# Attention through agents and a cosine layer, one core: first output products of a chunk one step later; in the last batch, half a step's copy behind the next cosine, linear products and the transposition's copy apart

## The chip, the cores and the metric

One of the cores of a Trainium2 chip runs the whole program. It has TensorE (PE, matrix products, written to PSUM), VectorE (DVE), ScalarE (ACT), GpSimd (POOL) and a queue that starts transfers (SP); each works through its own instructions in order and waits on semaphores for the others. GpSimd has no operand in PSUM anywhere in this kernel. The metric is the device time in microseconds (us) of one execution. Before the change it was 1162.13 us, the median of three runs (1161.17 to 1162.33).

## The reference

```python
scale = 1 / sqrt(128)                                   # B = 4 batches, N = 12480 tokens, C = 128
a2k   = softmax(scale * agents @ k.T)                   # 49 agents to all tokens
q2a   = softmax(scale * q @ agents.T)                   # every token to 49 agents
x     = (q2a @ (a2k @ v)).reshape(49920, 128)
h     = x @ w_in                                        # 128 -> 2048
out   = (h * cos(h)) @ w_out                            # 2048 -> 128
```

## The kernel before, in words

The 49920 tokens are 52 groups of 960 (`GRP`), 13 to a batch (`NG`), each of two chunks of 480 tokens (`CH`). For a chunk the 2048 inner columns are taken in 8 pieces of 256 (`NP` = 8), so there are 832 steps (`NSTEP`), 208 to a batch (`PER`). This text writes i = 0 to 7 for a step's place in its chunk and o for its place in its batch. What bounds the time is the loop over these steps (line 1165).

A step n does this. TensorE makes h for 256 columns, two products `ph<-pT,a` of 480 columns (line 1175; `a` already holds w_in multiplied by the agents' values, `pT` the tokens' softmax weights, transposed). ScalarE writes the cosine of it to `c` (line 1178). VectorE makes r = (c - 1) * h (line 1197), one instruction of 960 elements in each partition. Four steps later (`LAG` = 4) TensorE multiplies r by w_out, two products `po<-r,w` (line 1217), which add up over the chunk's 8 steps. Because r lacks h itself, the chunk's last step also adds two linear products `po<-pT,b` (lines 1213 and 1214). Then ScalarE copies the sum out, `osb<-po` (line 1226). So in the steps of the next chunk ScalarE's order is: cosine of i=3, the copy `osb<-po`, cosine of i=4.

Buffers: `ph` has three (line 618), so the h of a step may be made when the r of three steps before is done. `c` has three (`CB`), so a cosine waits until the readers of the cosine three steps before are done. `r` has six. `po` has one (line 624): the first product of a chunk waits until `osb<-po` of the chunk before has read it.

Beside this loop runs other work, which a planner puts into steps (`plan`, lines 1137 to 1153): scores of the next batch, values, projections, and in every step at most one such job on TensorE; the single buffer `one` takes their results. For each group `query_turned` (line 769) transposes the softmax weights: four products `one<-ident,p`, a copy `p<-one` on ScalarE (line 774), then on GpSimd two pairs `pT<-p` (a cast) and `pT<-p,pT` (a subtraction) for the two chunks.

In batches 0 to 2 these jobs fill TensorE and VectorE. The last batch has fewer of them. There, 23 steps (`asides`, line 1155; i = 0 of the batch's chunks, except near its two softmax bursts at o = 8 and o = 96) split their r: VectorE makes the first half (line 1190), ScalarE copies the second half of h out of PSUM to `raw` (line 1189), and GpSimd makes the second half of r from it in two instructions, a product and a subtraction (lines 1191 and 1192).

The order on each engine is the order of the code (`ordered`).

Of the kernel before, what the change touches and what calls it, by code (L numbers as in the profile page):

```python
# [9 lines left out]
F32 = mybir.dt.float32  # L10
F32R = mybir.dt.float32r
I32 = mybir.dt.int32
U32 = mybir.dt.uint32
AF = mybir.ActivationFunctionType
ALU = mybir.AluOpType
# [3 lines left out]
P = 128  # L19
# [3 lines left out]
CH = TT * HT  # L23
# [19 lines left out]
NV = 5  # L43
WL = 19
TL = 12
SH = 1
AD = 2
KB = 24
# [70 lines left out]
X1 = 208  # L119
XB = 1  # L120
XC = 3
XO = 1
N0 = 2
N1 = 4
N2 = 2
# [19 lines left out]
def agent_attention_cos_ffn(ctx, tc, qT, kT, v, agT, w_in, w_out, outT):  # L145
    nc = tc.nc
    NB, _, N = qT.shape
# [6 lines left out]
    NF = DFF // P  # L154
    NP = NF // 2
    NG = N // GRP
# [6 lines left out]
    looping = [False]  # L163
    wide_at = set()
    ordered = [False]
    step = [0]
    STEP = NCH * NP
    PER = NG * STEP
# [19 lines left out]
    pe, dve, act, pool = (Ordered(x) for x in (nc.tensor, nc.vector, nc.scalar, nc.gpsimd))  # L188
# [14 lines left out]
    w1 = const.tile([P, NF, P], F32R, name="w1")  # L203
# [412 lines left out]
    with ExitStack() as pools:  # L616
        sb = pools.enter_context(tc.tile_pool(name="sb", bufs=2))
# [3 lines left out]
        def small():  # L621
            return ps_1.tile([P, 512], F32, name="one")
# [11 lines left out]
        b1 = [sb.tile([KR, P], F32R, name=f"b1{i}", bufs=1) for i in range(2)]  # L634
        b2 = [sb.tile([KR, P], F32R, name=f"b2{i}", bufs=1) for i in range(2)]

        pTs = [sb.tile([KR, NCH, CH], F32R, name=f"pT_{i}", bufs=1) for i in range(3)]
# [19 lines left out]
        NSTEP = NB * PER  # L657
# [111 lines left out]
        def query_turned(n, lone=0):  # L769
            pt = small()  # L770
            for t in range(HT):
                pe.transpose(pt[:KR, t * TT:(t + 1) * TT], p_in[n % 2][:, t, :KR], ident[:TT, :TT])
            p = sb.tile([KR, CH], F32, name="p")
            act.copy(p, pt[:KR, :CH])
            pT = pTs[n % 3]
            for c, (own, other) in enumerate((half_rows, half_rows[::-1])):
                if lone:
                    act.copy(pT[own, c], p[own])
                else:
                    pool.tensor_copy(pT[own, c], p[own])  # L780
                (dve if lone else pool).tensor_sub(pT[other, c], p[own], pT[own, c].bitcast(F32))
# [223 lines left out]
        plan, post = Plan(), Plan()  # L1005
# [3 lines left out]
        def job(n, *parts, by=10 ** 6):  # L1009

            queue.append((n, len(queue), by, parts))
# [58 lines left out]
        for n in range(1, NQ):  # L1070
            plan(max(1, n * STEP - WL), query_weights, n)
            job(max(2, n * STEP - TL), (query_turned, n), by=n * STEP - TL + 6)

# [6 lines left out]
        early = [pieces[2 * b + 2] for b in range(NB)]  # L1080
# [3 lines left out]
        for b in range(NB):  # L1084
            o = b * PER
            go, stop = o + (T1 if b < NB - 1 else T3), o + PER + T2
# [28 lines left out]
            for g in range(NG):  # L1115
                plan(k1 + 16 + SH * g, nxt.shift, g, 1, pool)
            burst(go, early[b], late[b][:N1], nxt)
# [9 lines left out]
            i = (b + 1) % 2  # L1127
# [11 lines left out]
        while queue or begun:  # L1139
# [4 lines left out]
            x = min(ready, key=lambda x: (x[2], x[1]))  # L1144
            if x is not begun:
                queue.remove(x)
            n, i, by, parts = x
# [7 lines left out]
        def asides(n):  # L1155

            b, o = n // PER, n % PER
            if n < XA or n > NSTEP - 6 or any(x in shut for x in range(n - XB, n + XC)):
                return False
            if b == NB - 1:  # L1160
                return n % XL in XK and not T3 <= o < T3 + XZ
            return X0 <= o < X1 and n % XL in XP

        rs = {}
        for n in range(NSTEP + LAG):
            pinned[0] = n < NP
            looping[0] = True
            step[0] = n
            if n < NSTEP:
                q, c, i = n // STEP, n // NP % NCH, n % NP  # L1170
                ai = a[q // NG % 2]
                ph = ps_h.tile([P, 2, 512], F32, name="ph")
                for j in range(2):
                    f = slice((2 * i + j) * P, (2 * i + j + 1) * P)
                    pe.matmul(ph[:, j, :CH], ai[:, f], pTs[q % 3][:, c], start=True, stop=True)
                h = ph[:, :, :CH]
                cos = sb.tile([P, 2, CH], F32, name="c", bufs=CB)
                act.activation(cos, h, AF.Sin, bias=HALF_PI, scale=1.0)
                aside = asides(n)
                if aside and XO == 0:  # L1180
                    hs = sb.tile([P, 512, 2], U32, name="raw", bufs=2).rearrange("p x t -> p (x t)").bitcast(F32)[:, :2 * CH].rearrange("p (j x) -> p j x", j=2)
                    act.copy(hs[:, 0], h[:, 1])
            plan.run(n)
            if n < NSTEP:
                r = rs[n] = sb.tile([P, 2, CH], F32R, name="r", bufs=RB)
                if aside:
                    if XO:
                        hs = sb.tile([P, 512, 2], U32, name="raw", bufs=2).rearrange("p x t -> p (x t)").bitcast(F32)[:, :2 * CH].rearrange("p (j x) -> p j x", j=2)
                        act.copy(hs[:, 0], h[:, 1])
                    dve.scalar_tensor_tensor(r[:, 0], cos[:, 0], 1.0, h[:, 0], op0=ALU.subtract, op1=ALU.mult)  # L1190
                    pool.tensor_mul(hs[:, 1], cos[:, 1], hs[:, 0])
                    pool.tensor_sub(r[:, 1], hs[:, 1], hs[:, 0])
                elif TS and n == NSTEP - 1:
                    for j in range(2):
                        dve.scalar_tensor_tensor(r[:, j], cos[:, j], 1.0, h[:, j], op0=ALU.subtract, op1=ALU.mult)
                else:
                    dve.scalar_tensor_tensor(r, cos, 1.0, h, op0=ALU.subtract, op1=ALU.mult)
            while tails:
                f, args = tails.pop(0)
                f(*args)  # L1200
            post.run(n)
            m = n - LAG
            if m < 0:
                continue
            q, c, i = m // STEP, m // NP % NCH, m % NP
            if i == 0:
                if c == 0:
                    osb = sb.tile([P, GRP], F32, name="osb", bufs=2)
                po = ps_o.tile([P, 512], F32, name="po")[:, :CH]
            r = rs.pop(m)  # L1210
            if i == NP - 1:
                k = q // NG % 2
                pe.matmul(po, b1[k], pTs[q % 3][:, c], start=False, stop=False)
                pe.matmul(po, b2[k], pTs[q % 3][:, c], start=False, stop=False)
            for j in range(2):
                f = 2 * i + j
                pe.matmul(po, w1[:, f, :], r[:, j, :], start=(f == 0), stop=(f == NF - 1))
            if i == NP - 1:
                at = q * GRP
                if TS and m == NSTEP - 1:  # L1220
                    for on, copy, x in ((nc.sync, act.copy, 0), (nc.scalar, dve.tensor_copy, CH // 2)):
                        part = slice(c * CH + x, c * CH + x + CH // 2)
                        copy(osb[:, part], po[:, x:x + CH // 2])
                        on.dma_start(outT[:, at + part.start:at + part.stop], osb[:, part])
                    continue
                act.copy(osb[:, c * CH:(c + 1) * CH], po)
                if q == NQ - 1:
                    nc.sync.dma_start(outT[:, at + c * CH:at + (c + 1) * CH], osb[:, c * CH:(c + 1) * CH])
                elif c == NCH - 1:
                    nc.sync.dma_start(outT[:, at:at + GRP], osb)  # L1230
# [5 lines left out]
        pt = small()  # L1236
# [10 lines left out]
    with tc.If(far):  # L1247
        with ExitStack() as pools:
            sb = pools.enter_context(tc.tile_pool(name="gsb", bufs=2))
# [8 lines left out]
            p = sb.tile([TT, HT, 2 * HI], F32, name="p", bufs=1)  # L1258
# [64 lines left out]
            for b in range(NB):  # L1323
# [13 lines left out]
                for c in range(DFF // 512):  # L1337
# [5 lines left out]
                                                   op0=ALU.mult, op1=ALU.subtract)  # L1343
# [36 lines left out]
```

## Time and profile before

| what | us |
|---|---|
| median of the runs | 1162.13 |
| the profiled execution | 1160.97 |
| span in its trace | 1159.2 |
| TensorE busy | 1118.7 |
| VectorE busy | 1064.4 |
| ScalarE busy | 977.2 |
| GpSimd busy | 564.2 |

The span runs from the first instruction of the trace to the last; what lies around it is 1.8 us. A busy time counts an instruction from start to end, and two that overlap in an engine's pipeline are counted once. The granted clock of TensorE was 0.998 over the span.

### The profile page before, as it was taken

To read this page: it belongs to the slowest core of one execution; us is meant where nothing else is said; L and a number is where in the kernel's file an instruction comes from. 1 tells how busy PE (TensorE), PEld (TensorE's weight loads), DVE (VectorE), ACT (ScalarE), POOL (GpSimd) and SP (SyncE) were. 2 spreads that over 40 slices of the span, in tenths; PEclk is the share of its full clock that TensorE was granted. 3 is DMA by queue.
4 is the path that set the end of the run, shared out by engine and by line. 5 is a ranking of instruction groups with operands and counts; after the bars stand their busy time and mean duration, and the time that the engine had idled before them with its cause. 6 is when DMAs were issued, how large, how long until landed. Compare 5 with 4: busy or idle time off the path is not lost.

```text
span 1159.2 us, 17231 instructions
## 1 busy us (share of the span) xinstructions
PE 1118.7 (97%) x6075; PEld 924.1 (80%) x6075; DVE 1064.4 (92%) x1201; ACT 977.2 (84%) x1268; POOL 564.2 (49%) x726
## 2 busy tenths in 40 slices
PE   9989999999999999999999999999999999999996
PEld 8869888878887888877887888887888777767774
DVE  5888989999998999989999999998999899999996
ACT  3568877889889888898888887888988999999996
POOL 2013313678964122559893331366896455535551
PEclk9999999999999999999999999999999999999999
DMA  8734342143332232233331332224331100000001
GB/s 331 308 141 136 104 130 92 57 148 101 99 106 68 85 103 86 86 104 106 107 108 53 110 96 86 86 68 139 108 107 52 35 18 35 34 18 35 18 35 38
DMA packets 31631, 109.44 MB, mean 94 GB/s; under 512 B 3504, under 2 KB 4016, under 8 KB 31536
## 3 DMA queue, kind: packets, MB, share of 16 engines
q1 hardware_dynamic: 31392, 108.13, 28.7%
q8 instruction: 50, 0.82, 0.3%
q14 instruction: 45, 0.37, 0.1%
q10 hardware_dynamic: 144, 0.12, 0.0%
HBM read 82.68 MB, written 25.56 MB: 93 GB/s over the span
## 4 chain that ended last, share of the span: by engine, by line
PE 62%; DVE 21%; ACT 11%; issue 4%; POOL 1%; DMA 0%; ACTq 0%; DVEq 0%
PE ph L182 27%; PE po L182 23%; DVE r L182 15%; PE one L182 12%; ACT c L182 6%; DVE rz L182 2%; ACT osb L182 2%; DVE e L182 1%; DVE mx L182 1%; ACT p L182 1%; DVE sums L182 1%; ACT s L182 1%; ACT e L182 1%; ACT L182 1%; DVE s L182 1%
## 5 line engine op out<-in xcount | busy, mean ns | idle before, releaser
L182 DVE SCALAR_TENSOR_TENSOR r<-c,ph 128x960 fp32r<-128x960 f32 (+1 forms) x833 | 907.4, 1132 | 49.1 <-ACT c L182 41.8
L182 ACT ACTIVATE c<-ph 128x960 f32<-128x960 f32 x832 | 783.5, 977 | 132.8 <-PE ph L182 122.5
L182 PE MATMUL ph<-pT,a 113*128 113x480 f32 x1664 | 517.1, 392 | 16.3 <-DVE r L182 12.6
L182 PE MATMUL po<-r,w 128*128 128x480 f32 x1664 | 523.8, 396 | 5.6 <-ACT osb L182 5.3
L182 PEld LDWEIGHTS ph<-pT,a 113*128 113x128 f32 x1664 | 296.7, 189 | 123.0 <-DVE r L182 60.9
L182 PEld LDWEIGHTS po<-r,w 128*128 128x128 f32 x1664 | 291.8, 189 | 52.7 <-ACT osb L182 14.8
L182 POOL CAST pT<-p 49x480 fp32r<-49x480 f32 x102 | 59.2, 580 | 282.6 <-ACT p L182 279.8
L182 PEld LDWEIGHTS one<-ag,xt 128*120 128x120 f32 x1088 | 134.7, 184 | 11.3 <-DVE sums L182 1.5
L182 PE MATMUL one<-ag,xt 128*120 128x98 f32 x1088 | 134.2, 265 | 0.7 <-DVE b L182 0.4
L182 POOL TENSOR_TENSOR pT<-p,pT 49x480 fp32r<-49x480 f32 x102 | 124.1, 1217 | 8.2
L182 POOL TENSOR_TENSOR vh<-vt,vh 120x512 fp32r<-120x512 f32 x78 | 93.3, 1196 | 30.6 <-ACT vh L182 30.6
L182 POOL TENSOR_TENSOR p<-e,rz 120x392 f32<-120x392 f32 x51 | 43.5, 853 | 48.1 <-DVE rz L182 47.0
L182 PE MATMUL po<-pT,b 113*128 113x480 f32 x208 | 62.4, 381 | 0.0
L182 POOL TENSOR_TENSOR raw<-c,raw 128x480 f32<-128x480 f32 x23 | 28.3, 1229 | 70.0 <-ACT raw L182 69.9
L182 ACT COPY osb<-po 128x480 f32<-128x480 f32 x104 | 58.1, 559 | 2.2 <-PE po L182 2.2
L182 PEld LDWEIGHTS ph<-ag,xt 128*120 128x120 f32 x480 | 53.1, 188 | 7.5 <-DVE r L182 4.4
L182 PE MATMUL ph<-ag,xt 128*120 128x98 f32 x480 | 55.4, 272 | 3.1 <-DVE r L182 2.0
L182 POOL TENSOR_TENSOR e<-e,mx 120x392 f32<-120x392 f32 x26 | 21.9, 843 | 71.0 <-DVE mx L182 71.0
L182 PEld LDWEIGHTS one<-vh,eh 120*113 120x113 f32 x312 | 45.9, 177 | 8.2 <-POOL vh L182 2.5
L182 PE MATMUL one<-vh,eh 120*113 120x258 f32 x312 | 50.7, 284 | 1.4 <-DVE e L182 0.9
L182 POOL TENSOR_TENSOR eh<-s,eh 120x196 fp32r<-120x196 f32 x78 | 47.6, 610 | 6.3
L182 PEld LDWEIGHTS po<-pT,b 113*128 113x128 f32 x208 | 38.8, 188 | 6.0
(137 smaller groups left out, 725.4 us busy)
## 6 DMA issues: line engine op xcount, KB each, us to landing
xt<-qT SPq DMA_DIRECT2D x52, 480.0 KB, 3.5
outT<-osb SPq DMA_DIRECT2D x51, 480.0 KB, 2.8
xt<-kT SPq DMA_DIRECT2D x46, 480.0 KB, 3.7
vt<-v SPq DMA_DIRECT2D x43, 512.0 KB, 3.7
c<-kT SPq DMA_DIRECT2D x6, 480.0 KB, 6.9
vh<-v SPq DMA_DIRECT2D x5, 512.0 KB, 6.6
raw<-w_in SPq DMA_DIRECT2D x2, 512.0 KB, 6.5
a<-w_in SPq DMA_DIRECT2D x2, 512.0 KB, 5.7
```

Of the source, the lines that this page charges most:

```text
L182: ins = f(*args, **kw)
```

## The change

Four edits.

1. In all chunks but the very last (`early`), the output products of i=0 are left out in their own step and issued with those of i=1, one step later. In that later step the h products of the step come first, then four output products.
2. In the last batch (`even`), the two linear products no longer stand both at i=7: one goes ahead of the products of i=5 and one ahead of those of i=6. Of the deferred products of i=0 the first half goes with i=1, the second (GpSimd's half) with i=2.
3. In the split steps, ScalarE's copy of h moves behind the next step's cosine. GpSimd first subtracts 1 from the cosine (a `tensor_scalar`, which needs no h), and after the copy multiplies by h. VectorE's half no longer stands behind the copy.
4. In the last batch from o = 64 on (`TD`), the copy `p<-one` of `query_turned` and what follows it on GpSimd are issued two steps later than the four transposing products.

```diff
+            if looping[0] and step[0] >= NSTEP - PER + TD:
+                plan(step[0] + 2, query_turned_out, n, pt, lone)
+            else:
+                query_turned_out(n, pt, lone)
...
-                if aside and XO == 0:
...
+                while split_steps:
+                    hs, hb, rb = split_steps.pop()
+                    act.copy(hs[:, 0], hb[:, 1])
+                    pool.tensor_mul(rb[:, 1], hs[:, 1], hs[:, 0])
             plan.run(n)
...
                 if aside:
...
-                        act.copy(hs[:, 0], h[:, 1])
                     dve.scalar_tensor_tensor(r[:, 0], cos[:, 0], 1.0, h[:, 0], op0=ALU.subtract, op1=ALU.mult)
-                    pool.tensor_mul(hs[:, 1], cos[:, 1], hs[:, 0])
-                    pool.tensor_sub(r[:, 1], hs[:, 1], hs[:, 0])
+                    pool.tensor_scalar(hs[:, 1], cos[:, 1], 1.0, None, op0=ALU.subtract)
+                    split_steps.append((hs, h, r))
...
+            early = m < NSTEP - NP
+            even = early and q // NG == NB - 1
...
+            if even and i in (NP - 3, NP - 2):
+                pe.matmul(po, linear[i - (NP - 3)], pTs[q % 3][:, c], start=False, stop=False)
+            if i == 0 and early:
+                continue
+            if i == NP - 1 and not even:
+                for x in linear:
+                    pe.matmul(po, x, pTs[q % 3][:, c], start=False, stop=False)
+            todo = [(m, 0), (m, 1)]
+            if early and i == 1:
+                todo = [(m - 1, 0)] + ([] if even else [(m - 1, 1)]) + todo
+            if even and i == 2:
+                todo = [(m - 2, 1)] + todo
```

How it moves the instructions, at three places. In the names `w_70` is w_out, `pT_95` a group's transposed weights, `a_701` the folded w_in, `b_91` and `b_93` the linear products' weights.

TensorE in a middle batch, from the last products of a chunk to the first of the next, before:

```order
L182 MATMUL po<-r,w_70 128x480 x2
L182 MATMUL ph<-pT_95,a_701 128x480 [waits DVE_49]
L182 MATMUL ph<-pT_95,a_701 128x480
L182 MATMUL one<-vh_1972,eh_107 113x258 [waits Pool_49]
L182 MATMUL one<-vh_1972,eh_107 113x258 x3
L182 MATMUL po<-r,w_70 128x480 [waits Activation_49]
L182 MATMUL po<-r,w_70 128x480
L182 MATMUL ph<-pT_95,a_701 128x480 [waits DVE_49]
```

The same place after:

```order
L182 MATMUL po<-r,w_70 128x480 x2
L182 MATMUL ph<-pT_95,a_701 128x480 [waits DVE_49]
L182 MATMUL ph<-pT_95,a_701 128x480
L182 MATMUL one<-vh_1972,eh_107 113x258 [waits Pool_49]
L182 MATMUL one<-vh_1972,eh_107 113x258 x3
L182 MATMUL ph<-pT_95,a_701 128x480 [waits DVE_49]
L182 MATMUL ph<-pT_95,a_701 128x480
L182 MATMUL po<-r,w_70 128x480 [waits Activation_49]
L182 MATMUL po<-r,w_70 128x480 x3
```

The two products that wait for ScalarE's copy `osb<-po` stood ahead of the h products of i=5; now those come first, and four output products follow them.

TensorE in the last batch, from the chunk's last step (i=7 of its output products, which is i=3 of the next chunk's h) on, before:

```order
L182 MATMUL po<-pT_95,b_91 128x480
L182 MATMUL po<-pT_95,b_93 128x480
L182 MATMUL po<-r,w_70 128x480 x2
L182 MATMUL ph<-pT_95,a_701 128x480 x2
L182 MATMUL po<-r,w_70 128x480 x2
```

After, from two steps earlier:

```order
L182 MATMUL po<-pT_95,b_91 128x480
L182 MATMUL po<-r,w_70 128x480 x2
L182 MATMUL ph<-pT_95,a_701 128x480 x2
L182 MATMUL po<-pT_95,b_93 128x480
L182 MATMUL po<-r,w_70 128x480 x2
L182 MATMUL ph<-pT_95,a_701 128x480 x2
L182 MATMUL po<-r,w_70 128x480 x2
L182 MATMUL ph<-pT_95,a_701 128x480 x4
L182 MATMUL po<-r,w_70 128x480 x3
L182 MATMUL ph<-pT_95,a_701 128x480 x2
L182 MATMUL po<-r,w_70 128x480 x3
```

The linear products went one step apart to i=5 and i=6; the h products of i=4 and i=5 now follow each other with nothing between, and three output products stand behind each of the next two steps.

ScalarE in the last batch, from the copy of a chunk's sum (`osb<-po`) to the next, with a transposition's copy `p<-one` and a split step's copy `raw<-ph`, before:

```order
L182 COPY osb<-po 128x480 [waits PE_49]
L182 ACTIVATE c<-ph 128x960 [waits DVE_49,PE_49]
L182 COPY p<-one 113x480 [waits PE_49]
L182 ACTIVATE c<-ph 128x960 [waits DVE_49,PE_49] x4
L182 COPY raw<-ph 128x480
L182 ACTIVATE c<-ph 128x960 [waits DVE_49,PE_49] x2
L182 ACTIVATE c<-ph 128x960 [waits DVE_49,PE_49,Pool_49]
L182 COPY osb<-po 128x480 [waits DMAHW1_49,PE_49]
```

After:

```order
L182 COPY osb<-po 128x480 [waits PE_49]
L182 ACTIVATE c<-ph 128x960 [waits DVE_49,PE_49] x3
L182 COPY p<-one 113x480
L182 ACTIVATE c<-ph 128x960 [waits DVE_49,PE_49] x3
L182 COPY raw<-ph 128x480 [waits DVE_49]
L182 ACTIVATE c<-ph 128x960 [waits PE_49,Activation_49]
L182 ACTIVATE c<-ph 128x960 [waits PE_49,Pool_49]
L182 COPY osb<-po 128x480 [waits DMAHW1_49,PE_49]
```

`p<-one` went two cosines down, `raw<-ph` one. The cosine that waits for GpSimd is that of i=3, in both: it takes the buffer of the cosine of i=0, which GpSimd reads.

## Rows read from the trace of the kernel before

**Rows 1.** The page's busy times: engine, busy us, share of the span, instructions.

```profile
PE 1118.7 (97%) x6075; PEld 924.1 (80%) x6075; DVE 1064.4 (92%) x1201; ACT 977.2 (84%) x1268; POOL 564.2 (49%) x726
```

**Rows 2.** The page's chain that ended last: shares of the span by engine.

```profile
PE 62%; DVE 21%; ACT 11%; issue 4%; POOL 1%; DMA 0%; ACTq 0%; DVEq 0%
```

**Rows 3.** The windows view, 32 steps of the last batch: length, busy us (instructions), granted clock.

```profile
1050.46:1085.11 34.65, 33.94 (x146) 25.02 (x145) 33.11 (x33) 33.07 (x43) 18.64 (x18) 1.00 0.07 29
```

**Rows 4.** Groups on VectorE in that stretch: busy, mean ns | idle before, releaser.

```profile
L182 DVE SCALAR_TENSOR_TENSOR r<-c,ph 128x960 fp32r<-128x960 f32 x29 | 31.7, 1148 | 1.1 <-ACT c L182 0.9
L182 DVE SCALAR_TENSOR_TENSOR r<-c,ph 128x480 fp32r<-128x480 f32 x4 | 2.6, 653 | 0.5
```

**Rows 5.** The waits view, whole span: waiter <- waited for: us, times, longest.

```profile
ACT c L182 <- PE ph L182: 122.5, 268, 1.5
...
DVE r L182 <- ACT c L182: 41.8, 136, 1.8
...
PE ph L182 <- DVE r L182: 14.6, 45, 0.7
...
PE po L182 <- ACT osb L182: 5.3, 22, 0.5
```

**Rows 6.** The chain of waits in batch 2 near i=5 of a chunk: start, us, what.

```profile
861.06 1.07 DVE r L182
...
864.26 0.48 PE one L182 x4
864.74 0.44 PE po L182 x2
865.18 0.45 PE ph L182 x2
...
865.64 0.98 ACT c L182
```

**Rows 7.** The timeline of VectorE at three places: start, us, instruction, [idle before <- releaser].

```profile
739.27 1.16 DVE L182 SCALAR_TENSOR_TENSOR r<-c,ph 128x960 fp32r<-128x960 f32 x1 [0.54 <-ACT c L182]
...
866.65 1.15 DVE L182 SCALAR_TENSOR_TENSOR r<-c,ph 128x960 fp32r<-128x960 f32 x1 [0.17 <-ACT c L182]
...
1013.72 1.92 DVE L182 SCALAR_TENSOR_TENSOR r<-c,ph 128x960 fp32r<-128x960 f32 x2
1015.87 5.56 DVE L182 SCALAR_TENSOR_TENSOR r<-c,ph 128x960 fp32r<-128x960 f32 x5 [0.22 <-ACT c L182]
```

**Rows 8.** The timeline of ScalarE in the last batch, over two chunks.

```profile
1010.10 0.58 ACT L182 COPY p<-one 113x480 f32<-113x480 f32 x1
...
1013.53 0.98 ACT L182 ACTIVATE c<-ph 128x960 f32<-128x960 f32 x1 [0.22 <-PE ph L182]
1014.40 0.55 ACT L182 COPY raw<-ph 128x480 f32<-128x480 f32 x1
1014.84 2.75 ACT L182 ACTIVATE c<-ph 128x960 f32<-128x960 f32 x3
1017.48 0.55 ACT L182 COPY osb<-po 128x480 f32<-128x480 f32 x1
1017.92 0.99 ACT L182 ACTIVATE c<-ph 128x960 f32<-128x960 f32 x1
1019.26 2.73 ACT L182 ACTIVATE c<-ph 128x960 f32<-128x960 f32 x3 [0.36 <-PE ph L182]
```

**Rows 9.** The timeline of TensorE there, around the first product of a chunk.

```profile
1018.09 0.70 PE L182 MATMUL po<-r,w 128*128 128x480 f32 x2 [0.24 <-ACT osb L182]
```

**Rows 10.** The timeline of GpSimd there, from a transposition to a split step.

```profile
1010.74 0.58 POOL L182 CAST pT<-p 49x480 fp32r<-49x480 f32 x1 [1.83 <-ACT p L182]
...
1013.33 1.22 POOL L182 TENSOR_TENSOR pT<-p,pT 49x480 fp32r<-49x480 f32 x1
1015.10 1.22 POOL L182 TENSOR_TENSOR raw<-c,raw 128x480 f32<-128x480 f32 x1 [0.56 <-ACT raw L182]
```

**Rows 11.** A one-input group of GpSimd elsewhere in the program: busy, mean ns | idle before.

```profile
L182 POOL TENSOR_SCALAR a<-a 113x512 fp32r<-113x512 f32 x12 | 7.4, 615 | 24.8 <-ACT a L182 24.8
```

More of the change, by code (lines that the diff above doesn't have):

```diff
@@ L45 @@
 TL = 12
+TD = 64
 SH = 1
@@ L121 @@
 XC = 3
-XO = 1
 N0 = 2
@@ L772, in query_turned, with query_turned_out @@
                 pe.transpose(pt[:KR, t * TT:(t + 1) * TT], p_in[n % 2][:, t, :KR], ident[:TT, :TT])
+            if looping[0] and step[0] >= NSTEP - PER + TD:
+                plan(step[0] + 2, query_turned_out, n, pt, lone)
+            else:
+                query_turned_out(n, pt, lone)
+        def query_turned_out(n, pt, lone):
             p = sb.tile([KR, CH], F32, name="p")
@@ L1164, in agent_attention_cos_ffn @@
         rs = {}
+        split_steps = []
         for n in range(NSTEP + LAG):
@@ L1179, in agent_attention_cos_ffn @@
                 aside = asides(n)
-                if aside and XO == 0:
-                    hs = sb.tile([P, 512, 2], U32, name="raw", bufs=2).rearrange("p x t -> p (x t)").bitcast(F32)[:, :2 * CH].rearrange("p (j x) -> p j x", j=2)
-                    act.copy(hs[:, 0], h[:, 1])
+                while split_steps:
+                    hs, hb, rb = split_steps.pop()
+                    act.copy(hs[:, 0], hb[:, 1])
+                    pool.tensor_mul(rb[:, 1], hs[:, 1], hs[:, 0])
             plan.run(n)
@@ L1186, in agent_attention_cos_ffn @@
                 if aside:
-                    if XO:
-                        hs = sb.tile([P, 512, 2], U32, name="raw", bufs=2).rearrange("p x t -> p (x t)").bitcast(F32)[:, :2 * CH].rearrange("p (j x) -> p j x", j=2)
-                        act.copy(hs[:, 0], h[:, 1])
+                    hs = sb.tile([P, 512, 2], U32, name="raw", bufs=2).rearrange("p x t -> p (x t)").bitcast(F32)[:, :2 * CH].rearrange("p (j x) -> p j x", j=2)
                     dve.scalar_tensor_tensor(r[:, 0], cos[:, 0], 1.0, h[:, 0], op0=ALU.subtract, op1=ALU.mult)
-                    pool.tensor_mul(hs[:, 1], cos[:, 1], hs[:, 0])
-                    pool.tensor_sub(r[:, 1], hs[:, 1], hs[:, 0])
+                    pool.tensor_scalar(hs[:, 1], cos[:, 1], 1.0, None, op0=ALU.subtract)
+                    split_steps.append((hs, h, r))
                 elif TS and n == NSTEP - 1:
@@ L1209, in agent_attention_cos_ffn @@
                 po = ps_o.tile([P, 512], F32, name="po")[:, :CH]
[L1210 to L1217, printed above, removed]
+            early = m < NSTEP - NP
+            even = early and q // NG == NB - 1
+            k = q // NG % 2
+            linear = (b1[k], b2[k])
+            if even and i in (NP - 3, NP - 2):
[10 more added lines that the diff above has]
+                todo = [(m - 2, 1)] + todo
+            for x, j in todo:
+                f = 2 * (x % NP) + j
+                pe.matmul(po, w1[:, f, :], rs[x][:, j, :], start=(f == 0), stop=(f == NF - 1))
+                if j:
+                    rs.pop(x)
             if i == NP - 1:
```

## Prediction

> **What bounds the kernel now.** I read the busy times first [rows 1]: TensorE is busy for 97% of the span, VectorE for 92%, ScalarE for 84%. No engine has room for much, and no one of them is the bound all along. The chain that ended last says the same [rows 2]: 62% of it runs over TensorE, 21% over VectorE, 11% over ScalarE. The waits come next [rows 5]. The waits that the change is aimed at are small: TensorE's output products wait for the copy `osb<-po` 5.3 us in all, in 22 places, and r waits for a cosine 41.8 us in 136 places.
>
> Then I read stage by stage. In the middle batches the chain at a chunk's fifth cosine reads: a job on TensorE, two output products (0.44 us), the h products, the cosine, then r [rows 6]. VectorE idles there, 0.17 us at this place and 0.54 us at another [rows 7]. This chain piece stands 21 times in batches 0 to 2 at i=5. In the last batch the windows view counts 34.65 us for 32 steps, 8.66 us a chunk, with 33.11 us of VectorE, 33.07 us of ScalarE and 33.94 us of TensorE [rows 3]. All VectorE's idle time there is 1.1 + 0.5 us in four chunks [rows 4], so 0.4 us a chunk is the most that any edit can win there, unless VectorE gets less work, and it gets none less.
>
> **Edit 1, middle batches.** Nothing is added: the same products in another order. The h products of i=5 come one pair of output products earlier, 0.44 us, in 21 places: 9.2 us is the upper end. Little of it stays. It stays where VectorE idles before that r and nothing else ends later afterwards. The example: r starts at 866.65 after 0.17 us of idle time [rows 7]; with its cosine 0.44 us sooner VectorE is simply continuous, so 0.17 us is won. Where the idle time is 0.54 us the whole 0.44 us is won. I find per batch one place of the second kind (the chunk ending near o = 77, where the next batch's maximum is taken) and three of the first (near o = 109, 141, 173). At the other visits the four output products and the next job on TensorE stand ahead of a later cosine, and this one comes at the same time as before, since the sum of TensorE's work up to it is the same. So 0.44 + 3 x 0.17 = 0.95 us a batch, three batches: -2.9 us. The lower end is 0.
>
> What covers the cost: four products in a row stand ahead of the h of i=6, which then starts two pairs, 0.87 us, after those of i=5 end. Where VectorE is the bound, that cosine has about half a microsecond to spare, so I take no cost.
>
> **Edits 2 and 3, last batch, a chunk without a transposition.** I laid the chunk out by hand from the trace, with t = 0 at 1013.72, the start of the r before the split step [rows 7], a cosine every 0.87 us where ScalarE is continuous (three in 2.75 us, of which the last has its full 0.99 [rows 8]), and an r every 1.07 us (the chain's piece for one [rows 6]; one lasts 1.148 us, so 0.08 us overlaps with the next, and a half of 0.653 us [rows 4] holds the next up by 0.58). Before: the half r starts at 1.27 (it waits for the end of `raw`, 1014.40 + 0.55 [rows 8]), the next r at 2.15 after 0.22 us of idle time [rows 7], the r of i=7 at 8.69. After: the half r starts at 1.07, as VectorE comes free. The cosine of i=1 starts at 0.88 and its r at 1.89, 0.26 us sooner than before. But the copy now stands from 1.76 to 2.31 before the cosine of i=2, which starts at 2.19 rather than 1.99, so the r of i=2 starts at 3.20 where VectorE would have been free at 2.96. Before, it started at 3.22. The stall is moved by one step, not removed, since the copy costs ScalarE its 0.44 us in either place and both places have a late cosine behind them. What is left is the end of TensorE's wait for `osb<-po` (0.24 us [rows 9]) and of the late cosine behind it (0.36 us idle [rows 8]). The r behind it was late by only 0.04 us. In all 0.05 us a chunk is won, with 0 and 0.4 us as ends. Of the 23 split chunks 13 are of this kind: -0.65 us.
>
> **A chunk whose transposition's copy is not moved.** At o = 20, 36 and 52 the copy `p<-one` still stands behind the cosine of i=4. That cosine comes later than before, at 4.41 rather than 4.20 (1017.92 in [rows 8]). ScalarE now idles about 0.2 us before the cosine of i=1, whose h isn't there yet; the copy `raw` filled that gap before, and now follows it. So the cosine of i=5 comes 0.22 us later too, and there VectorE waits for it: 3 x 0.22 = +0.66 us.
>
> **Edit 4, and what is queued behind it.** `p<-one` starts at about 7.1 in its chunk instead of 5.1. ScalarE has room for it there. But GpSimd's four instructions on `pT` follow it in order, and behind them stands the split step's subtraction of the next chunk. Before, the four began at 1010.74, 0.06 us after the copy's end, and ended at 1013.33 + 1.22, so they take 3.81 us, and the split step's first instruction came 0.55 us later [rows 8, 10]. It then waited for `raw`, not for GpSimd. After: the copy ends at 7.68, GpSimd's four run from 7.74 to 11.55, which is 2.9 in the next chunk (8.64 long). Then the subtraction runs, 0.6 us, to 3.6. The cosine of i=3 needs the buffer that this instruction reads, and wants to start at 3.08 (2.19 + 0.87, and a little for the handing over). It is 0.5 us late. Behind it on ScalarE stand the copy `osb<-po` and the cosines of i=4 and i=5; on TensorE the first products of the next chunk wait for that copy. r of i=3 starts 0.33 us late, r of i=4 and all that follow 0.48 us late, and VectorE has no idle time left to take it back. A split step follows a moved transposition 7 times (o = 72, 88, 120, 136, 152, 168, 184): 7 x 0.48 = +3.4 us. The price of the subtraction is open, since GpSimd has none of this shape in the trace. The ends are 0.58 us, the cast on `pT` [rows 10], and 1.22 us, the two-input product on `raw` of the same shape [rows 10]. I take 0.6, since the one-input form on 512 elements takes 0.615 us [rows 11]. With 1.22 us the term becomes 7 x 1.1 = +7.7 us. At the other end, were the four on `pT` over by 2.4, the term would be 0.
>
> **The sum** is made against the profiled execution, 1160.97 us: -2.9 - 0.65 + 0.66 + 3.4 = +0.5, 1161.5 us. The median of the runs lies 1.16 us above that execution, so I forecast 1162.6 us.
>
> **Rivals.** Faster: GpSimd's lateness doesn't decide, because a real chunk leaves the cosine of i=3 later than my 3.08 anyway, or GpSimd starts earlier than 7.74; then +3.4 falls away, and the middle batches keep a third of the 9.2 us. 1162.1 - 2.9 - 0.65 + 0.66 gives 1159.2; with half of the 9.2 us kept and 0.2 us a chunk in the last batch (13 chunks) it is 1162.1 - 4.6 - 2.6 = 1154.9. For it: VectorE's 41.8 us of waits on cosines [rows 5], far more than I spend. Against: most of them stand in steps full of TensorE's jobs.
>
> Slower: GpSimd's chain decides more than I say. The place is the cosine of i=3 in the 7 chunks behind a moved transposition, the price is one for one with each tenth that the subtraction ends later than 3.08. With 1.22 us for it: 1162.6 + 4.3 = 1166.9. For it: the only GpSimd instruction of this exact shape takes 1.22 us. Against: it reads two tiles; those that read one are near 0.6 [rows 10, 11].
>
> Slower, by the clock: edit 2 leaves TensorE without output products between the h of i=4 and of i=5, so it pauses where it had been fed. The granted clock in the last batch is 1.00 with TensorE busy 33.94 of 34.65 us [rows 3], the higher of its two levels, 2.4 GHz. Were it to fall to 1.2 GHz for one chunk in four of the 23, each losing its 34 products of some 0.22 us once more less the chunk's slack of 0.2 us, that would be 6 x 7 = 42 us. The Trainium skill, "TensorE: Matmul & The Clock Gate", section "A second HAM failure mode: psum-queue depth-cycling", tells of a kernel in which small pauses between groups of products made the clock go back and forth between the levels. By that rule this rival would hold, and the time would be near 1204 us; the trace here speaks against it, since VectorE makes TensorE wait for 14.6 us in all as it is [rows 5] and the granted clock over the span is still 0.998.
>
> No effect: each edit moves a wait to where another ends at the same time. That is 1162.1, inside my own range.
>
> **How the numbers follow.** About 0.2%, 2.3 us, is what a measurement of this kernel can tell from no change. Chances: my sum 0.44 (its own range 1159.8 to 1164.8), no effect 0.07, faster rival 0.27, GpSimd's rival 0.20, clock 0.02. My sum with its spread counts 0.35 within the bound, 0.05 on the faster side and 0.04 on the slower. The faster rival counts 0.25 faster and 0.02 within; GpSimd's 0.18 slower and 0.02 within; no effect counts as same; the clock as slower. So faster 0.30, same 0.46, slower 0.24. The range reaches to the middle of the faster rival's numbers and to the slower one: 1156.5 to 1167.
>
> **What would show it.** In the profile after, in the last batch: the cosine of i=3 behind a moved transposition released by GpSimd (a new wait of ScalarE for `raw`, 7 times, near 0.5 us; none, and edit 4 is free); VectorE idle before r of i=1 and i=2, near 0.24 us each, and none before the half r; GpSimd's subtraction near 0.6 us; TensorE's wait for `osb<-po` nearly gone. In the middle batches: VectorE's idle time before r at i=5 less by some 3 us. I am wrong if the last batch's chunk comes out far from 8.6 us, or if the middle batches shorten by over 5 us.

## The result: slower by 0.55%

The changed kernel took 1167.49 us (median of 8 runs), the kernel before 1161.88 us beside it (8 runs). The ratio of the runs is 1.0055, with a 95% interval of 1.0044 to 1.0065. Forecast were 1162.6 us within 1156.5 to 1167, so the time lies half a microsecond above the range, on the side of the slower rival.

The profiled execution of the changed kernel took 1168.34 us, its span is 1166.6 us. Its busy times and the chain that ended last, the answer to [rows 1, 2]:

```profile
PE 1117.1 (96%) x6075; PEld 923.5 (79%) x6075; DVE 1065.0 (91%) x1201; ACT 982.3 (84%) x1268; POOL 568.6 (49%) x726
...
PE 56%; DVE 23%; ACT 12%; issue 5%; POOL 3%; DMA 1%; SPq 0%; POOLq 0%; ACTq 0%; DVEq 0%
```

The busy times are nearly what they were: ScalarE's grew most, by 5.1 us, and GpSimd's by 4.4. GpSimd's share of the chain grew from 1% to 3%, and TensorE's fell from 62% to 56%. The waits view of the changed kernel, whole span, against [rows 5]:

```profile
ACT c L182 <- PE ph L182: 106.8, 238, 1.3
...
DVE r L182 <- ACT c L182: 49.6, 164, 1.8
...
PE ph L182 <- DVE r L182: 23.2, 58, 1.2
...
ACT c L182 <- POOL raw L182: 8.5, 7, 1.2
...
PE po L182 <- ACT osb L182: 5.9, 8, 0.7
```

The last line but one did not stand there before: ScalarE's cosine waits for GpSimd's `raw`, 7 times, 8.5 us. The wait of TensorE for `osb<-po` has fewer places, 8 instead of 22, and is no shorter in all.

Where the time went is read by stage. I compared when the first cosine of each group starts in the two traces. The changed kernel enters the loop 2.20 us late, in code that is the same (below). It leaves batch 2 2.20 us ahead: the middle batches won 4.4 us. It reaches the last step 7.75 us late: the last batch lost 9.95 us. The two make +5.55 us, against 5.61 between the medians. 32 steps of the last batch, and VectorE's groups in them, against [rows 3, 4]:

```profile
1064.16:1101.39 37.23, 34.63 (x145) 24.57 (x144) 33.31 (x33) 33.74 (x42) 19.35 (x18) 1.00 0.07 27
```

```profile
L182 DVE SCALAR_TENSOR_TENSOR r<-c,ph 128x960 fp32r<-128x960 f32 x29 | 32.2, 1151 | 3.9 <-ACT c L182 3.8
L182 DVE SCALAR_TENSOR_TENSOR r<-c,ph 128x480 fp32r<-128x480 f32 x4 | 2.6, 648 | 0.0
```

The stretch, which holds two places behind a moved transposition, is 37.23 instead of 34.65 us long. VectorE's idle time before r went from 1.6 to 3.9 us; before the half r it is gone, as edit 3 meant it. The granted clock is 1.00, as before.

One chunk behind a moved transposition, on GpSimd, then ScalarE, then VectorE:

```profile
1072.09 0.58 POOL L182 CAST pT<-p 49x480 fp32r<-49x480 f32 x1 [4.07 <-ACT p L182]
1072.75 1.22 POOL L182 TENSOR_TENSOR pT<-p,pT 49x480 fp32r<-49x480 f32 x1
1074.01 0.58 POOL L182 CAST pT<-p 49x480 fp32r<-49x480 f32 x1
1074.67 1.22 POOL L182 TENSOR_TENSOR pT<-p,pT 49x480 fp32r<-49x480 f32 x1
1075.98 1.41 POOL L182 TENSOR_SCALAR raw<-c 128x480 f32<-128x480 f32 x1
```

```profile
1074.78 0.56 ACT L182 COPY raw<-ph 128x480 f32<-128x480 f32 x1
1075.24 0.98 ACT L182 ACTIVATE c<-ph 128x960 f32<-128x960 f32 x1
1077.43 0.97 ACT L182 ACTIVATE c<-ph 128x960 f32<-128x960 f32 x1 [1.21 <-POOL raw L182]
1078.30 0.55 ACT L182 COPY osb<-po 128x480 f32<-128x480 f32 x1
```

```profile
1074.91 1.15 DVE L182 SCALAR_TENSOR_TENSOR r<-c,ph 128x960 fp32r<-128x960 f32 x1 [0.17 <-ACT c L182]
1076.25 1.15 DVE L182 SCALAR_TENSOR_TENSOR r<-c,ph 128x960 fp32r<-128x960 f32 x1 [0.18 <-ACT c L182]
1078.43 1.15 DVE L182 SCALAR_TENSOR_TENSOR r<-c,ph 128x960 fp32r<-128x960 f32 x1 [1.03 <-ACT c L182]
1079.76 2.22 DVE L182 SCALAR_TENSOR_TENSOR r<-c,ph 128x960 fp32r<-128x960 f32 x2 [0.17 <-ACT c L182]
```

The cosine of i=3 starts 0.03 us after GpSimd's `TENSOR_SCALAR` ends, 1.21 us after ScalarE was free. VectorE idles 1.03 us before the r of i=3 and 0.17 us before the next. The two smaller stalls of 0.17 and 0.18 us stand before r of i=1 and i=2. The instruction on GpSimd takes 1.41 us, where the prediction had put 0.6.

The length of a chunk, from the start of the r of i=7 to the same of the next chunk, in us (differences of start times on VectorE's timeline; at o = 160 lies a transposition, the chunk at o = 168 comes behind it):

| kernel | o = 160 | o = 168 |
|---|---|---|
| before | 8.66 | 8.68 |
| changed: edits 1 to 4 | 8.69 | 9.92 |
| e1: without edit 4 | 8.95 | 8.69 |
| e2: changed, GpSimd's instruction at 0.59 us | 8.69 | 9.11 |
| e3: edit 1, middle batches | 8.67 | 8.66 |
| e4: edit 4 alone | 8.74 | 10.07 |
| e6: edits 1 and 2 | 8.90 | 8.65 |
| e7: edits 1 (middle batches) and 3 | 8.95 | 8.95 |
| e8: edit 1, all batches | 8.65 | 8.63 |

### The profile page after: what moved, and what is told of

It is laid out like the page before. It is cut to its first block, busy times and chain, and to the rows that moved or that the text cites. A ratio compares the mean times of both kernels' runs of the same rounds, so it can differ in the third digit from the quotient of the medians.

```text
span 1166.6 us, 17255 instructions
## 1 busy us (share of the span) xinstructions
PE 1117.1 (96%) x6075; PEld 923.5 (79%) x6075; DVE 1065.0 (91%) x1201; ACT 982.3 (84%) x1268; POOL 568.6 (49%) x726
## 4 chain that ended last, share of the span: by engine, by line
PE 56%; DVE 23%; ACT 12%; issue 5%; POOL 3%; DMA 1%; SPq 0%; POOLq 0%; ACTq 0%; DVEq 0%
PE ph L182 24%; PE po L182 21%; DVE r L182 17%; PE one L182 11%; ACT c L182 7%; POOL pT L182 2%; DVE rz L182 2%; ACT s L182 1%; POOL raw L182 1%; ACT L182 1%; ACT e L182 1%; ACT p L182 1%; DVE mx L182 1%; ACT osb L182 1%; DVE e L182 1%
## 5 line engine op out<-in xcount | busy, mean ns | idle before, releaser
L182 PE MATMUL ph<-pT,a 113*128 113x480 f32 x1664 | 523.9, 396 | 24.2 <-DVE r L182 21.2
L182 PE MATMUL po<-r,w 128*128 128x480 f32 x1664 | 499.1, 391 | 6.2 <-ACT osb L182 5.9
L182 PEld LDWEIGHTS ph<-pT,a 113*128 113x128 f32 x1664 | 289.6, 189 | 130.5 <-DVE r L182 68.2
L182 PEld LDWEIGHTS po<-r,w 128*128 128x128 f32 x1664 | 298.4, 189 | 52.0 <-ACT osb L182 9.6
L182 PE MATMUL po<-pT,b 113*128 113x480 f32 x208 | 66.3, 380 | 0.0
L182 POOL TENSOR_SCALAR raw<-c 128x480 f32<-128x480 f32 x23 | 32.5, 1413 | 57.3 <-PE ph L182 49.7
```

What stands on the lines that cost most here:

```text
L182: ins = f(*args, **kw)
```

## The experiments

The theory: of the 9.95 us of the last batch 8.8 are GpSimd's lateness behind a moved transposition, some 1.25 us in each of 7 places, and it is that long since its one-input instruction takes 1.41 us. Rivals: the late copy of edit 3, or TensorE's pauses by edit 2, cost by themselves, and GpSimd's wait only shows it.

**e1, edit 4 taken back.**

```diff
-TD = 64
+TD = 1000
```

> The changed kernel with edit 4 taken back (the transposition's copy stays in its step; edits 1 to 3 remain). Theory: the loss is the cosine of i=3 behind a moved transposition, held up by GpSimd, 1.28 us in each of 7 pairs of chunks; without edit 4 GpSimd is done near 2.3 us into the chunk, before that cosine starts at 3.1, so these 9.0 us go, and each of the 7 chunks with a transposition costs about 0.3 us, as the four unmoved ones did: 1167.5 - 9.0 + 7 x 0.3, about 1160.5 us, and no wait of ScalarE for raw. Rival, edit 3's copy or edit 2's pause on TensorE is what costs, and GpSimd's wait only shows it: the time stays above 1165 us.

Measured: 1161.19 us, ratio to before 0.9996 [0.9986, 1.0005]. ScalarE waits nowhere for `raw` any more, and the chunk behind a transposition falls from 9.92 to 8.69 us. The chunk with the transposition rises from 8.69 to 8.95 us, about as much as three of the four unmoved ones had risen. So edit 4 is what makes the chunk behind it slow, and it does win 0.26 us in its own chunk. The last batch of this run is still 3.4 us longer than before: without edit 4, edits 2 and 3 use up most of what edit 1 wins in the middle batches.

**e2, a shorter instruction on GpSimd.** Half of r is another function here.

```diff
-pool.tensor_scalar(hs[:, 1], cos[:, 1], 1.0, None, op0=ALU.subtract)
+pool.tensor_scalar(hs[:, 1], cos[:, 1], 1.0, -1.0, op0=ALU.min, op1=ALU.max)
```

> The changed kernel with GpSimd's subtraction replaced by the two-operation form (a minimum, then a maximum) that lasts 0.615 us on 113x512 elsewhere in the program; with it half of r in the split steps is not computed as in the reference. Theory: the subtraction's 1.41 us is a matter of the operation, so this one lasts near 0.6 us, the wait at the cosine of i=3 falls from 1.28 to about 0.48 us a pair, and the time is 1167.5 - 7 x 0.8, about 1162 us. Rival: the instruction lasts 1.4 us by what it reads and where (a cosine buffer that VectorE reads at the same time, 128 partitions, an output in full precision), whatever the operation: still 1.4 us and 1167.5 us.

Measured: 1161.97 us, 0.9997 [0.9989, 1.0006]. GpSimd's group and the wait in the last batch:

```profile
L182 POOL TENSOR_SCALAR raw<-c 128x480 f32<-128x480 f32 x23 | 13.5, 588 | 57.4 <-PE ph L182 48.4 <-ACT c L182 8.1
```

```profile
ACT c L182 <- POOL raw L182: 2.7, 7, 0.4
```

The chunk behind a moved transposition takes 9.11 instead of 9.92 us: 0.81 us less for an instruction that is 0.82 us shorter. The price is one for one, as the slower rival of the prediction said, and at 0.59 us the loss is 0.43 us (9.11 against 8.68), where the prediction had put 0.48.

**e3 and e9, edit 1 alone in batches 0 to 2.** The new code of edit 1 on the kernel before:

```diff
-            early = m < NSTEP - NP
+            early = m < NSTEP - PER
```

> The kernel before with edit 1 alone, and only in batches 0 to 2; the last batch is as before. Theory: VectorE's idle time before r at i=5 falls, and the three batches shorten by the 4.4 us seen between the two profiles: 1161.9 - 4.4, about 1157.5 us. Rival: the 4.4 us are partly drift of one profile (its first stretch, in code that is unchanged, was 2.2 us longer), and the blind sum's 2.9 us or less holds: 1159 us or more.

> Edit 1 in batches 0 to 2 alone, once more, beside the version with it in all batches: 1157.1 us as before if the gain is real, within half a microsecond.

Measured: 1157.1 us, 0.9963 [0.9950, 0.9976], and in the second run 1157.93 us, 0.9968 [0.9958, 0.9977]. In the first one's trace the three batches are 4.36 us shorter and the last batch is unchanged to 0.05 us. The second run's trace has the three batches 4.29 us shorter. The gain of edit 1 is real.

**e4, edit 4 alone**, on the kernel before; GpSimd's product and subtraction of a split step both follow the copy `raw`, as before.

```diff
+            if looping[0] and step[0] >= NSTEP - PER + TD:
+                plan(step[0] + 2, query_turned_out, n, pt, lone)
+            else:
+                query_turned_out(n, pt, lone)
```

> The kernel before with edit 4 alone. Theory: with the split steps as before, GpSimd's first instruction of a split step also stands behind the four on pT, which end 2.9 us into the next chunk; its 1.23 us then end at 4.2, where the cosine of i=3 wants to start at 2.9: 1.3 us in each of 7 places, 1161.9 + 9, about 1171 us. Rival: edit 4 costs only together with edit 3 (the longer subtraction); alone it is free or wins a little, 1161 to 1162 us.

Measured: 1174.02 us, 1.0105 [1.0089, 1.0120]. On the kernel before, the move costs more, not less: the chunk behind takes 10.07 us. At o = 72 and two other places of the 7 it is 10.9 to 11.3 us. At all 7 TensorE waits 1.64 to 1.68 us for `osb<-po`; at these three the wait is followed by a lower clock. The timeline of TensorE at the first of them, then two stretches of the windows view there, then two around the wait of 1.67 us at 1065.35, one of the other four:

```profile
1003.02 0.78 PE L183 MATMUL po<-r,w 128*128 128x480 f32 x2 [1.68 <-ACT osb L183]
1003.60 1.00 PE L183 MATMUL ph<-pT,a 113*128 113x480 f32 x2
```

```profile
1000.00:1003.60 3.60, 1.92 (x10) 1.22 (x8) 2.71 (x3) 2.32 (x4) 3.44 (x4) 0.99 0.00 0
1003.60:1006.80 3.20, 3.20 (x10) 2.63 (x8) 2.42 (x3) 1.78 (x3) 0.00 (x0) 0.50 0.00 0
...
1063.00:1066.00 3.00, 1.33 (x7) 0.87 (x6) 2.11 (x2) 2.12 (x3) 2.84 (x3) 1.00 0.00 0
1065.90:1069.00 3.10, 3.04 (x14) 2.33 (x13) 2.75 (x4) 2.74 (x4) 0.02 (x1) 1.00 0.00 0
```

At the first place TensorE was busy for 1.92 of 3.60 us, and the granted clock then was 0.50, the lower level of 1.2 GHz, for the next 3.2 us. At the other, after a wait as long, it stayed at 1.00. What decides between them no run here shows. The Trainium skill, "TensorE: Matmul & The Clock Gate", section "A second HAM failure mode: psum-queue depth-cycling", tells of such changes of level by small and frequent pauses. Here the pause ahead of each fall was single and long, while the changed kernel, whose waits for `osb<-po` are 0.7 us each, kept 1.00. The three chunks are together 3.2 us longer than the other four of the 7 would make them; the theory's 1171 us was 3 us too low.

**e5, six forms of the one-input instruction** in turn over the 23 split steps, without edit 4; three of them make another function of half of r.

```text
form 0: tensor_scalar(..., 1.0, None, op0=subtract)          form 1: (..., -1.0, None, op0=add)
form 2: (..., 1.0, -1.0, op0=min, op1=max)                   form 3: (..., 1.0, None, op0=min)
form 4: (..., 1.0, 1.0, op0=subtract, op1=mult)              form 5: (..., -1.0, -1.0, op0=add, op1=max)
```

> The changed kernel without edit 4, in which GpSimd's one-input instruction of the 23 split steps takes six forms in turn, all on the same 128x480 tiles: minus 1; plus -1; minimum then maximum; minimum alone; minus 1, then times 1; plus -1, then maximum. The third, the fourth and the sixth change half of r in those steps. Two theories on the 1.41 us. By the number of operations: the forms with one operation last 1.41 us, those with two 0.59 us, whatever the operations are. By the operation: the forms with a subtraction or an addition last 1.41 us and those with minimum or maximum alone 0.59 us, or the subtraction alone is slow and the addition is not. Whatever form is exact and near 0.6 us is the price that the prediction had taken.

One execution, 1161.38 us. Form 5, then forms 0 to 4 in order on GpSimd's timeline:

```profile
1097.10 1.82 POOL L182 TENSOR_SCALAR raw<-c 128x480 f32<-128x480 f32 x1 [4.68 <-PE ph L182]
1106.13 1.42 POOL L182 TENSOR_SCALAR raw<-c 128x480 f32<-128x480 f32 x1
1114.74 1.42 POOL L182 TENSOR_SCALAR raw<-c 128x480 f32<-128x480 f32 x1 [5.08 <-PE ph L182]
1123.76 0.59 POOL L182 TENSOR_SCALAR raw<-c 128x480 f32<-128x480 f32 x1
1132.37 1.42 POOL L182 TENSOR_SCALAR raw<-c 128x480 f32<-128x480 f32 x1 [5.88 <-PE ph L182]
1141.06 1.83 POOL L182 TENSOR_SCALAR raw<-c 128x480 f32<-128x480 f32 x1 [5.90 <-PE ph L182]
```

Neither theory is right as it stood. One operation takes 1.42 us, a minimum as much as a subtraction; two take 1.83; the pair minimum and maximum takes 0.59. That pair is the one form of `TENSOR_SCALAR` that the kernel before has on GpSimd [rows 11], so the nearest row was an exception. The 23 instructions agree within 0.01 us for each form. No form tried here that computes the reference's r is near 0.6 us.

**e6, edits 1 and 2 alone.** The new code of products on the kernel before, nothing else.

> Edits 1 and 2 alone, on the kernel before: the split steps and the transposition's copy as they were. Theory: batches 0 to 2 win their 4.0 to 4.4 us; in the last batch the end of TensorE's wait for the copy osb takes the 0.04 us from before r of i=5 in a chunk, nothing else, so -4.2 - 23 x 0.04, about 1157 us, like edit 1 in the middle batches alone (1157.1). Rival: edit 2 is what costs the 0.03 us a plain chunk and 0.29 us a chunk with an unmoved transposition in the run without edit 4 (1161.2); then 1160 to 1161 us.

Measured: 1160.36 us, 0.9986 [0.9977, 0.9995]. The rival was right for edit 2: a chunk with a transposition takes 8.90 us, one without 8.65. ScalarE's timeline there:

```profile
1006.78 2.11 ACT L182 ACTIVATE c<-ph 128x960 f32<-128x960 f32 x2
1008.79 0.55 ACT L182 COPY osb<-po 128x480 f32<-128x480 f32 x1
1009.22 0.99 ACT L182 ACTIVATE c<-ph 128x960 f32<-128x960 f32 x1
1010.09 0.58 ACT L182 COPY p<-one 113x480 f32<-113x480 f32 x1
1010.53 1.88 ACT L182 ACTIVATE c<-ph 128x960 f32<-128x960 f32 x2
```

From `osb` to the cosine of i=5 ScalarE is continuous, so a late cosine of i=3 goes through to r of i=5, where VectorE idles 0.17 us. The cosine of i=3 starts 1.16 us ahead of its r (1.41 in the kernel before). Its h stands behind the linear products that edit 2 put into the two steps before. That these are the cause is read from the trace; e8 below, which has them at i=7, agrees, but it also leaves out the other half of edit 2.

**e7, edit 1 in the middle batches and edit 3.** The changed kernel with `TD = 1000` and the change of e3.

> Edit 1 in batches 0 to 2 and edit 3, on the kernel before: the products of the last batch as they were, the transposition's copy not moved. Theory: the late copy raw is what shifts the cosines of i=3 and i=4 and costs 0.3 us where a transposition's copy follows, so the time is that of the run without edit 4, about 1161 us, or longer, since TensorE now also waits for the later copy osb. Rival, edit 2 costs: about 1157 us, as edit 1 in the middle batches alone.

Measured: 1164.06 us, 1.0024 [1.0013, 1.0034]. From o = 64 on every split chunk but those at the burst takes 8.95 us, with a transposition or without. The rival, that edit 2 alone costs, has fallen: edit 3 costs by itself, 0.29 us in a plain chunk. With edit 2 it costs 0.03 there (8.69 in e1). The likely reason, from the traces, is TensorE's wait for `osb<-po`: in the last batch it stands in 13 places of some 0.25 us in e7, and in one in e1. So edit 3 needs edit 2 in a plain chunk. In a chunk with an unmoved transposition each costs 0.24 to 0.29 us alone, and the two together no more (e1).

**e8, edit 1 alone in all batches**, with the linear products at i=7 and both halves of i=0 deferred together (`even = False`).

> Edit 1 alone, in all four batches (both halves of the deferred products go with i=1, the two linear products stay at i=7). Theory: the shift of the linear products ahead of the h of i=2 and i=3 is what cost 0.24 us a chunk with a transposition; without it the last batch keeps its 8.66 us a chunk, or wins the 0.04 us before r of i=5 in each of some 20 chunks: 1157.1 - 0.8, about 1156.3 us, and not over 1157.1. Rival, deferring the products in the last batch costs by itself (three or four products in a row ahead of the h of i=6): 1158.5 us or more, with chunks of 8.9 us.

Measured: 1158.31 us, 0.9964 [0.9951, 0.9977]. Chunks of the last batch take 8.65 and 8.63 us, and the trace has that batch 0.68 us shorter than before. The chunks of 8.9 us that the rival named did not come. In the time, which is above the 1157.1 us that the theory allowed, this can't be told from e3 and e9. It, e3 and e9 beat both kernels; e3 has the lowest median, 1157.1 us.

## Why the prediction was wrong

- **Edit 4, the step that failed: "I take 0.6".** The mechanism, the 7 places and the way the price passes on were right; the term was mis-sized. The subtraction lasts 1.41 us, above both ends that were set for it, 0.58 and 1.22 [rows 10]. By the prediction's own working 1.41 us gives 7 x (0.48 + 0.81) = 9.0 us; measured are 8.8 (7 x 1.25). e2 shows the price one for one. With this term the sum would have been 1168.2 us, within 0.7 us of the measurement; that closeness is partly luck, since edit 1 won 1.5 us more than forecast and the rest of the last batch lost 1.15 us where nothing in all was forecast (-0.65 + 0.66).
- **How that happened.** The one-input price was read from a `TENSOR_SCALAR` of nearly the same size [rows 11], without asking which operations it has. They are a minimum and a maximum (line 519), and e5 shows that pair to be the exception. And the upper end was taken to be the two-input instruction, as if a single input could only be cheaper.
- **Edit 1: right, and too small.** Forecast -2.9, measured -4.4 us. At the four places named per batch the chunks are shorter by 0.43 (o = 72), 0.15, 0.24 and 0.22 us, 1.04 for the 0.95 forecast. At o = 72 VectorE's idle time before r of i=5 fell from 0.54 to 0.10 us, and at the others VectorE is now continuous [rows 7]. The rest are places passed over: one chunk of batch 0 (o = 24) won 0.45 us, and smaller ones 0.1 to 0.2. On the chain the piece of [rows 6] now reads, in the changed kernel, a job, then the h products at once:

```profile
862.26 0.48 PE one L182 x4
862.74 0.43 PE ph L182 x2
863.17 0.86 PE po L182 x4
```

- **Edits 2 and 3 in a plain chunk.** Forecast -0.05, measured +0.03 us. The stall did move by one step: 0.17 and 0.18 us before r of i=1 and i=2, where 0.24 each were forecast. That edit 3 without edit 2 loses 0.29 us there (e7), and edit 2 without edit 3 0.24 us in a chunk with an unmoved transposition (e6), was not seen. TensorE's wait for `osb<-po` did nearly go, as forecast, in e1 (0.7 us in one place); in the changed kernel 7 of its 8 places are those behind a moved transposition.
- **Unmoved transpositions, and the rest of the last batch.** Forecast were +0.22 us each at o = 20, 36 and 52. In the changed kernel the chunk at o = 32 is 0.27 us longer and those at o = 48 and 56 together 0.29, but the chunk at o = 16 is 0.18 us shorter. Not forecast were +0.29 us in the chunk at o = 0, which also has a transposition, and +0.20 and +0.30 us in the last two chunks; why these two are longer is not shown.
- **The clock.** No change of level in the changed kernel's loop, as thought likely; e4 shows that the level can fall in this loop: it did after three of seven waits of 1.64 to 1.68 us.

## What to carry to other kernels

A row prices another instruction only if its operations are the same, not only its name and shape; where they differ, the upper end has to lie above every form seen, not at the dearest neighbour. When an instruction is moved later, what counts is the whole queue behind it on the next engine: here four instructions of GpSimd stood in front of a fifth, which had to read the cosine of i=0 before the cosine of i=3 could take its buffer. And edits that go together should each be timed alone: edit 1 won 4.4 us in the middle batches, and the four together lost 9.95 in the last.

## What the runs showed of the hardware that was not expected

- GpSimd's `TENSOR_SCALAR` on 128x480: 1.42 us with one operation (subtract, add or minimum), 1.83 with two (subtract and multiply, add and maximum), 0.59 with minimum and maximum, beside 1.22 us for a two-input product.
- The same wait of TensorE did not always have the same consequence for the clock. In e4 three waits of seven, all 1.64 to 1.68 us, were followed by the lower level. In e1 and e5 TensorE waits 1.53 and 1.54 us for r at the burst at o = 104; the clock stayed at 1.00 in e1 and fell to 0.50 in e5, where this chunk takes 10.79 instead of 9.68 us.
- The time from the start to the first step of the loop, in code that no kernel here changed, was between 0.23 (e5) and 6.87 us (e8) longer than in the profile of before. In e8's trace one stretch of it ran at the lower clock:

```profile
40.00:50.00 10.00, 10.00 (x51) 10.00 (x51) 6.23 (x13) 2.18 (x5) 0.00 (x0) 0.52 1.03 414
```

So a single profile's total is uncertain by microseconds. Chunks of the loop with the same code nearly all agree to 0.06 us between the traces (one, at o = 112 of batch 0, to 0.23), save where the clock fell; differences of one or two microseconds were read from the chunks.
